# A fused gated linear attention and MLP kernel: another written-out order of its steps

## The chip, the core and the metric

The kernel runs on one core of one Trainium2 chip. The metric is the device time of one execution in microseconds (us). Five engines work side by side, each with its own in-order queue: TensorE (PE) for matrix products, VectorE (DVE) and ScalarE (ACT) for elementwise work, GpSimd (POOL) for small elementwise work, and SyncE (SP), which here issues all DMA transfers. PE takes two instructions for a product, a weight load (PEld) and the product itself (PE); a float32 product takes two such pairs, a bfloat16 product one. A float32 transpose also shows one pair in this kernel's trace.

## What is computed

The reference has two parts. The first is a gated recurrence over 768 tokens, for 4 batches of 8 heads with 48 channels; the second is an MLP with a leaky activation over the resulting 3072 rows.

```python
mag = np.sqrt(a_re * a_re + a_im * a_im)
scale = np.minimum(mag, 0.999) / (mag + 1e-06)
a_re_n, a_im_n = (a_re * scale, a_im * scale)
for t in range(S):
    ar, ai = (a_re_n[:, :, t, :, None], a_im_n[:, :, t, :, None])
    new_re = ar * S_re - ai * S_im
    new_im = ar * S_im + ai * S_re
    kv = np.einsum('bhd,bhe->bhde', k[:, :, t], v[:, :, t])
    S_re, S_im = (new_re + kv, new_im)
    y[:, :, t] = np.einsum('bhd,bhde->bhe', q[:, :, t], S_re)
...
h = x @ w_in                     # x: (3072, 384), w_in: (384, 2048)
g = np.maximum(h, 0.0) + alpha * np.minimum(h, 0.0)
return (g @ w_out).astype(np.float32)   # w_out: (2048, 384)
```

Inputs and output are float32 in the reference's shapes; x is y with its heads laid side by side.

## The kernel before

**Units.** A unit is 128 tokens of one batch with all eight heads. There are 24 units, six for each batch, numbered in order of time within the batch. The recurrence is solved inside a unit by six levels of halving (half lengths 1, 2, 4, ..., 32), and between units by a state St that is passed on.

**Gates.** The function `gates` (nine calls, for one unit, two units, and then three units each) turns the gate inputs into magnitudes ("dec", stored to DRAM as decs) and into products of unit phases ("phs"). It is a long chain of DVE and ACT steps (L251 to L308), of complex products (L336 and L338, small ones of batches 1 to 3 on POOL), and of the last products (L422, L425), which are stored as phs (L427).

**Loads.** `loads` brings KQ (queries and keys of a unit, L575 and L577), PP (its phases, L586) and T (its decays, L593). KQ has three buffers, T two, PP one. `half_rows` and `loads_v` bring the values: a copy to DRAM in another layout (vsc, L556), V (L602 to L607) and VL (L625, L628), with one buffer each.

**A unit's steps** (`unit`). DVE rotates KQ with PP (L648). For each level PE makes 16 small products into ps_lv (`meet`, L662), DVE scales KQ with T for the next level (L701) and masks the result into A (L686, or ACT at L683), and ACT copies half of the keys into W (L719). After the last level PE transposes the keys (L736), ACT copies them (L738), and PE makes the products for the state (ps_kv, L747). Then follow the products for the output ps_y: four bfloat16 products with zeros, which clear the unit's sum (L759), 48 products with A (L768), and, once the state is known, 16 products with St (L793). DVE updates St (L777, L780). ACT copies ps_y (L807) and SP stores it as ysc (L812).

**The MLP** (`all_mlp`). Units are taken in 14 groups: two of one unit, ten of two, two of one. `loads_x` brings a group's rows back as xT (L825). For each of 16 feature blocks, `features` makes three products into ps_h (L841), ACT applies Relu (L848), and DVE adds alpha (L850), which also frees the ps_h buffer (two there are). `outputs` makes one product per unit and feature block into ps_o (L860); after the sixteenth ACT copies it (L870) and SP stores it (L873). Both weights are loaded in sixteen pieces and converted on ACT and DVE (`pieces`, L487; `to_f32`, L503 to L515).

**What sets the order.** Every function above is a generator that stops (`yield`) ahead of each of its steps. A string, ORDER, has one letter for each step, 4,316 in all. The run goes through it and advances the generator that the letter names by one step, so the string alone decides in which sequence every engine's queue is filled:

```python
def run(self, order):
    for c in order:
        next(self.tasks[self.LETTERS.index(c)], None)
```

A to I are the nine gate chains, J loads, K half_rows, L loads_v, M pieces, N and O the weights in and out, P to Z and a to m the 24 units, n loads_x, and o the MLP. The arguments of each `yield` (a cost, what it waits for, which buffers it takes, and for PE a number n of product instructions) were meant for the planner that composed the string; in this kernel they do nothing. That of the step which clears a unit's sum counts 12 products and four clearing ones:

```python
ev = yield PE(0.335 if s or part else 0.44, ..., mode=2, n=12 if s or part else 14)
if not (s or part):
    ...
            nc.tensor.matmul(..., lhsT=nothing[64 * i:64 * i + 64], rhs=ident.bitcast(BF16)[64 * i:64 * i + 64],
                             start=True, stop=False)
```

The waits between engines follow from the data and from the buffers; the order changes none of them, only what stands ahead of what.

Of the kernel before, what the change touches and what calls it, by code (L numbers as in the profile page):

```python
# [27 lines left out]


ORDER = (  # L30
    "AAAAAAAAAAABBBAAAAAAAAAMMMMMJKKNJAAABBNAAAMNNAANKJJAOAAAAAAAAAAAAAAABAAKKKKKKKOBLLAANAAAAAAAOOMLAAAA"
    "BBOKLLLMAAABALABLKBBAAAKAAABBNAABABAAABAABAAAAABBBBBBABABAABNNABBBBBABAABBBBBBBBBBBBOOOBBBNBBNBBBBBN"
    "BMBOBJBBBJPCNNBBCBBBBBBBCOBBBBBBPOBPPBCBLLJJOCONBNBCBMPJJJBJMBOBBLBNBOPBBPBPPBPBBOCCCPCPPCOCPCJJJPPP"
    "PCCPPCCOOJCLOPPLLCOPPCPPCCNDJNCCJNNDPQQDMPPPCMOCOKCPPPPPPPPNCCCCOCJJCMCCNCCCCCCPPKKCJCCQDDCCCCPCQCDC"
    "CPCPPPQPQPPPPKCJNJNCNNCKQCCNCNDOCJCRCCQCCNCDDDCONOOCRQNRCRQQCPQQQCDJKDCCORQCKQDDQCOKCQCCDNCKKQQMCDOQ"
    "nODCLLLLLLLLLQLLQQRLLDCJDOCDMDQoDDKCQCoMoKKKDCLCCCOQQQJQQQDQRQDCQQCQRKJDDDRDDCDCCCCQCOQOCOOOQDoQNDND"
    "oRoooooDMKRDoRRDNDoOooQNDJREoooooJoNRSDQRooRQRRoJNoLLoDoQoooooRJoSQLLERRRDRRooooooDLQLOSLLLNRRDLLLDD"
    "DLDRoooooLDDESSODoESRooRSEooQNQENRoSoNooooooRRRRRRRoSSNRoMRoDoEooSSROOOOooORoooNDNDoODDDNRooDDoDDDDR"
    "JoooJNKJRJJSoooJnTEooooooooooSoLLDTDDDDESSSEoooooooJJJJLLLSSSJJSSJooDJLLooSoooRTooooooDDDLLSooooLLDD"
    "DDDDoLETTDSooTRoSSLKKSooUooooooEoESoooSREELSoSKKKDoTooooooSEoERSKSSSSSDoSooooLDDDSDLDEoDToJLLEDTJLLL"  # L40
    "EooDDDooLooEooooSooSDSSSSSETUToSLooToooLoooDEEoooEEoTLTooooToEoooooToooLLDTToooDTTTTooDnLoooTEEooooD"
    "TUoooToUEDTooooUTToEoooooUTUTJUEEEEEooUoJoEoTJoooUTTJTTTTTTEooTFJUTEFooooooKooTJUUUoULUoooEooEULEooL"
    "LUTUUUUEoULLLLoooUoELoToUUUoEEoEEVEEEooEEEEEFEUVUoLJULooooLTLUJTUVToVVVUUUUUUUUVFVVVooooooVVVVooJoVo"
    "JoJTTUJJUJWVVJLUUUEEEEEEEEEEEEoEoooVJFoJoVooWVUUWooLLLLLLLLWWVoLLLLVEooWWEVoVVVWooooVVWWVoooWVVooVoL"
    "EEVEVonJJoVVVEJVFWVVJWoVEEEEEFFoVJWVoWWFFEKWJJooooLooVVooFXEFJJWEEWooooLLLLLooooWEFWELLLLJELLLWoEEEV"
    "VVVVVWEoooooooWoWWoXoWooooLEWWEWEooooooooWEEooooKWWWWWWJEFXXXXWLWFJXXoooWLLoJoooXLoLFWFFoWWJXXXXLFFo"
    "oooooooJWoooooLLWWFWFLLXFLLFLFLFFXYooooooooXXoWWoooFFFoooXXYoFYXXFFoooXXoooXGooXXFXYFFooooooXXXooYFF"
    "FFFoooXXooooYnXFXFoFoFGFXXXXXoooXoXooYYooJJJoJJJZooYJXXXYJLYXXXFFFJFFXLFFooYYooooFJFZZYYZFKXLYoooooo"
    "oooooZZYYZYFFFFFFYYYoLFLLLZZLLFFFFLFFYFYooooKKooooooYZFoGLYYooYoLLLYJYoJooZYYooFYYFJYYZYYYYKFFFFFJZF"
    "ZYaZGGFFFooZooooooooFoLLooooFoJooooJYFGFZZFFFFYYYYYYYFFaZaoooooFGoooaJZJKJoaGFLooZZFFooooooZZoaoLLaL"  # L50
    "GZZoooooooFLKoFGGGooZZaaZoZoooooGooooGooZoLLLZaGLLaFaoooaGoGGooGoooooJLLZZZZZZZaaHnooooKoGGGGGGGGGGH"
    "aooooaHJJLLLLLLKoooooZZLGGGZaaaGaaaaLLooooooooGGooooKoooHLLLZZGGZZGZZZaboooooooaaJooLooHoGGboaaHaGoG"
    "GoooooJJGooooGooJJaoabHbaaGGabbbJaaGaGGGGGGGGHbJaboHHJbJJooooooGooGcbbbbHHHooooboooooHaaaaaabbHbbGGo"
    "GooaaoooooooobccbooHobbJJGooooooocbboccbobobboobGoHbGGGGGGGGGGbGccoobooobcoHLLLJLLLLLLLLLLLbbbbbbcbc"
    "cGobboooooJGncJJdooLLGLooLcGLooooooGGGGodccccccHooccooccLLKGLGbbbJJLLoLcobbccbbcbooLGooooGGGdccooooo"
    "oooGGGccGGooooLLoooooocJGdcooHcccHGocGHGJJLLdHHHHHLLcHccHoooLodooJooLooddooGooooHHHHHodooooodIdccccH"
    "HooHHHoooooooooHcoddcooooJJocoHdoododHoooHddddHdeddJodooooooLLooooJIoIdeoooLdeeddddeoooooodLcLLooLdL"
    "dneooeeoooooeddddIdKKddHHHHHHHHHdddeoIddeooeooddIJJJJJJfdJJLoeJoooILHHHHHooooLLLLoeooJIIeLLLLLeIoooo"
    "oooeeeffoooooooeeeeeKKooooffefoHeoHoHHeHHHHHHHHHHHfoHeIoHHeoeooIefeLLJfLIIIIIIIIoodoJoHoeeeeeeeoooHJ"
    "JooeeHoooooeegfIKooooHffHfoooooooofJHHHJJJfIfoeeeeeeogfLIooJooooooJfoHHHofoooIooHggHffHHoofffnHogooo"  # L60
    "ooogHLLLLLLLLLLLfffKKHLLHooofoooHHofoooooooooooIIoIffIoIHfooffffHKfKooooofggogoooofffgffLJogJoogohLo"
    "gooohgJJoggoooooooooooooooooooooogLhhLLfggggggffohhhLLoKoooooooogoooooohggIJJooooogJgghhgJoooJhogooL"
    "LLhhLLLhgfgggggJggKffIooohiooooooohgJgIIIiggoggggIIooooIIIIooooooooIIIIIJiooooohiioohoooJIJJJooJoooo"
    "ooooooooLooonoihhooooohhihhoooohhoooooIooIIIIIIIIIIooooooLIIIIIIIIIIIIIIILoLIooLoiihiohiooooohhhhooo"
    "ohiLLLhLJiooLLLLLhhhhhhojohhhIoooooIoIIiiooioooLoLiLiiiiijhhiLJiJLLLjjooLIIIIIIILojILLLoooooijjjoojL"
    "IIILoioIooIoooojooiiIiooiioooojjoioooooooohhhIoojohiiiiiiiiiihhiiiiLLLLLLjIjiojooooioijLLLjIIjIoooIj"
    "jnjoJooLLIjoooooJJJJJLjoooojooooooooooooooooooLjooooojjooojooojooojoooLJJookojojjjjjJjjjjjkkoooookko"
    "oookokooooJJkoJooJJJkkkjJjLLlookkjoooookkkkooooooollkolkLkLLLkklkjoooooooLokojlkkLLLLoLoLLkoookJkooo"
    "kllkolllkkkkkJkkkkkJJJlojooooooljkkJJkoLkLkklolooolkolookJooomooooooooooolllnLLommmmoolllLooooLooooo"
    "ooooooooooooooooLLLLLmmllllloooooooooooloooooolmmoololoooLLLoooooooooooolmoooooooooollllmmlmlmmlmlll"  # L70
    "mLLoooooooooLLooLLolmLLLooLLLlloooooloLomoooooooooooooommmmmmmoommooooooooollnooooooomoomooooooooooo"
    "ooooooooooooommooooooooooooooooooooooooooooooooooooooommmmmmmmmmmmmmmoooooooooooooonoooooooooooooooo"
    "oooooooooooooooooooooooooooooooooooooooooooooooooooooooooooooooooooooooooooooooooooooooooooooooooooo"
    "oooooooooooooooo")

# [877 lines left out]
```

## Time and profile before

| | |
|---|---|
| median of 3 runs | 878.04 us (871.34 to 885.96) |
| the profiled execution | 879.98 us, span 878.3 us |
| PE busy | 712.8 us (81%) |
| DVE busy | 648.2 us (74%) |
| ACT busy | 425.8 us (48%) |
| POOL busy | 167.5 us (19%) |
| mean granted clock of PE | 0.955 |
| DMA | 130.92 MB in 194,559 packets, mean 149 GB/s |
| largest groups | L841 308.0 us, L860 298.4 us, L701 176.8 us |

A page of the profile has the busy time of each engine, then 40 equal slices of the span in which a digit is the busy share in tenths, then the DMA queues, and then groups of instructions by source line ("L841" is line 841). A group's row names the engine, the operation, what is written and read, the count, the busy time, the mean of one in ns, and the idle time just before it with what ended it. "X <- Y" in a row of waits means that X was released by Y; three numbers follow, the sum in us, how often, and the longest. "issue" as the releaser means that nothing the profile shows was waited for. The queue named "instruction" carries the engines' own programs.

### The profile page before, as it was taken

The page shows a single profiled execution, that of the slowest core. Times are in us where ns is not written, and L with a number is a line of the kernel's source. Part 1 is how long each engine was busy: PE and PEld are TensorE (multiplying, and loading weights), DVE is VectorE, ACT ScalarE, POOL GpSimd, SP SyncE. Part 2 cuts the span into 40 slices and gives each one's busy share as a digit, 9 for nine tenths or more (in the row PEclk, how much of TensorE's full clock was granted, in tenths as well). Part 3 has the DMA queues.
Part 4 walks back from the last instruction along what each step waited for, and adds up shares of the span by engine and source line. Part 5 has one row for each costly group of instructions (what it writes and reads, how often), then busy time and mean ns, then how long its engine had stood idle before and what let it go on. Part 6 is the DMA issues. An engine that isn't in the chain of part 4 may idle for free.

```text
span 878.3 us, 26867 instructions
## 1 busy us (share of the span) xinstructions
PE 712.8 (81%) x11488; PEld 534.3 (61%) x11488; DVE 648.2 (74%) x1012; ACT 425.8 (48%) x913; POOL 167.5 (19%) x277
## 2 busy tenths in 40 slices
PE   0001325788979998979999999999999979999998
PEld 0001324567757776757776776777777766777776
DVE  5999999888977998769987896885756737624212
ACT  7587693666344653536673446543334314233121
POOL 3000002363132310520073105810032000000000
PEclk9999755999998999999999999999999999999999
DMA  8698869886984989447976678659544392712010
GB/s 225 187 240 201 229 155 286 191 169 124 252 165 88 172 181 235 102 94 203 213 139 132 166 187 158 135 153 212 119 90 98 92 212 47 157 31 65 10 38 9
DMA packets 194559, 130.92 MB, mean 149 GB/s; under 512 B 74504, under 2 KB 186248, under 8 KB 194440
## 3 DMA queue, kind: packets, MB, share of 16 engines
q1 hardware_dynamic: 194440, 129.20, 64.6%
q8 instruction: 90, 1.47, 0.7%
q14 instruction: 29, 0.24, 0.1%
HBM read 100.82 MB, written 35.71 MB: 155 GB/s over the span
## 4 chain that ended last, share of the span: by engine, by line
PE 63%; DVE 9%; DMA 8%; ACT 5%; issue 4%; SPq 3%; POOL 2%; DVEq 0%; POOLq 0%; ACTq 0%
PE ps_h L841 25%; PE ps_o L860 25%; PE ps_lv L662 4%; PE ps_y L768 3%; PE ps_y L793 2%; DVE KQ L701 2%; PE ps_kv L747 2%; DMA PP<-phs 2%; SPq L625 1%; PE ps_kt L736 1%; DMA T<-decs 1%; DMA VL<-vsc 1%; DMA g_sb<-in_w_in_dram 1%; POOL gate L336 1%; DMA phs<-gate 1%
## 5 line engine op out<-in xcount | busy, mean ns | idle before, releaser
L841 PE MATMUL ps_h<-xT,w_in_sb 128*128 128x256 f32 (+1 forms) x1344 | 308.0, 360 | 5.6 <-DVE g_sb L850 5.1
L860 PE MATMUL ps_o<-w_out_sb,g_sb 128*128 128x384 f32 x768 | 298.4, 502 | 10.3 <-DVE g_sb L850 10.1
L841 PEld LDWEIGHTS ps_h<-xT,w_in_sb 128*128 128x128 f32 x1344 | 234.2, 195 | 76.9 <-DVE g_sb L850 7.5
L701 DVE TENSOR_TENSOR KQ<-KQ,T 96x1024 f32<-96x1024 f32 x144 | 176.8, 1235 | 58.9 <-PE ps_lv L662 55.6
L850 DVE SCALAR_TENSOR_TENSOR g_sb<-g_sb,al,ps_h 128x256 f32<-128x256 f32 (+1 forms) x224 | 97.2, 436 | 135.8 <-ACT g_sb L848 135.6
L848 ACT ACTIVATE g_sb<-ps_h 128x256 f32<-128x256 f32 (+1 forms) x224 | 78.7, 352 | 243.9 <-PE ps_h L841 242.8
L860 PEld LDWEIGHTS ps_o<-w_out_sb,g_sb 128*128 128x128 f32 x768 | 139.1, 193 | 61.1 <-DVE g_sb L850 11.8
L719 ACT COPY W<-KQ 96x512 f32<-96x512 f32 x120 | 74.7, 624 | 70.3 <-DVE KQ L701 62.0
L662 PE MATMUL ps_lv<-KQ,W 96*32 96x32 f32 x3840 | 57.2, 205 | 49.9 <-ACT W L719 44.4
L662 PEld LDWEIGHTS ps_lv<-KQ,W 96*32 96x32 f32 x3840 | 44.8, 117 | 78.2 <-ACT W L719 51.0
L648 DVE TENSOR_TENSOR KQ<-KQ,PP 96x2048 f32<-96x2048 f32 x24 | 55.2, 2300 | 10.4 <-DMA PP<-phs 5.1
L662 PE MATMUL ps_lv<-KQ 96*32 96x32 f32 x768 | 12.2, 208 | 62.1 <-DMA VL<-in_v_dram 51.3
L768 PE MATMUL ps_y<-A,VL 64*48 64x64 f32 x2304 | 44.4, 226 | 21.5 <-issue 18.7
L336 POOL TENSOR_TENSOR gate<-gate 128x72 f32<-128x72 f32 x42 | 25.6, 609 | 160.9 <-ACT gate L366 158.1
L768 PEld LDWEIGHTS ps_y<-A,VL 64*48 64x48 f32 x2304 | 41.1, 127 | 23.4 <-issue 20.0
L662 PEld LDWEIGHTS ps_lv<-KQ 96*32 96x32 f32 x768 | 9.7, 120 | 66.2 <-DVE KQ L648 51.8
L336 DVE TENSOR_TENSOR gate<-gate 128x576 f32<-128x576 f32 (+5 forms) x84 | 47.6, 566 | 1.6
L683 ACT ACTIVATE A<-ps_lv,rows 128x64 f32<-128x64 f32 x144 | 40.0, 330 | 16.0 <-PE ps_lv L662 15.6
L807 ACT COPY yT<-ps_y 48x256 f32<-48x256 f32 x96 | 32.0, 365 | 30.9 <-PE ps_y L793 24.7
L422 DVE TENSOR_TENSOR gate<-gate 128x1152 f32<-128x1152 f32 (+2 forms) x36 | 43.5, 1218 | 0.4 <-POOL gate L407 0.3
L686 DVE TENSOR_TENSOR A<-ps_lv,mask 128x256 f32<-128x256 f32 x96 | 39.4, 413 | 0.0
L738 ACT COPY KT<-ps_kt 128x384 f32<-128x384 f32 x48 | 22.9, 478 | 24.5 <-PE ps_kt L736 24.3
(100 smaller groups left out, 771.8 us busy)
## 6 DMA issues: line engine op xcount, KB each, us to landing
T<-decs SPq DMA_DIRECT2D x48, 384.0 KB
PP<-phs SPq DMA_DIRECT2D x48, 193.5 KB
KQ<-in_q_dram SPq DMA_DIRECT2D x48, 192.0 KB
decs<-gate SPq DMA_DIRECT2D x7, 1152.0 KB
phs<-gate SPq DMA_DIRECT2D x14, 576.0 KB
KQ<-in_k_dram SPq DMA_DIRECT2D x40, 192.0 KB
vsc<-in_v_dram SPq DMA_DIRECT2D x48, 144.0 KB
VL<-vsc SPq DMA_DIRECT2D x24, 288.0 KB
```

The lines of the kernel that those rows point to most:

```text
L336: on(4 * k).tensor_tensor(out=m, in0=w[:, 1::-1].unsqueeze(2).to_broadcast([P, 2, 2, k]), in1=pairs_of(u), op=ALU.mult)
L422: TT(out=m[:, a], in0=U5[:, 1 + a], in1=turned(off3, o)[:, a].unsqueeze(1).unsqueeze(3).to_broadcast([P, L // 2, nb, 2]), op=ALU.mult)
L648: nc.vector.tensor_tensor(out=KQ, in0=KQ, in1=bass.AP(tensor=PP.tensor, offset=PP.offset, ap=[PP.ap[0], (1, 2), (P + 1, H), (1, P)]), op=A ...
L662: nc.tensor.matmul(t[64 * i + j:64 * i + j + HC // 2, p], lhsT=weights(4 * i + p)[:, j:j + HC // 2], rhs=q_[:, m * g:m * (g + 1)], start=T ...
L683: nc.scalar.activation(a[:, :, cols], t[:, :, at:at + name], AF.Copy, scale=s)
L701: nc.vector.tensor_tensor(out=x, in0=x, in1=m, op=ALU.mult)
L719: nc.scalar.copy(W.rearrange("p n t -> p (n t)").rearrange("p (m h) -> p m h", h=h), halves(KQ[:, 1].rearrange("p n t -> p (n t)"), h)[:, ...
L768: nc.tensor.matmul(o, lhsT=Vp[h][64 * i:64 * i + 64, s, e_ * D:(e_ + 1) * D], rhs=a, start=False, stop=False)
L841: nc.tensor.matmul(p, lhsT=w_in_sb[:, f // 2, kk, f % 2 * P:(f % 2 + 1) * P], rhs=x_of[m][:, kk], start=(kk == 0), stop=(kk == NK - 1))
L848: nc.scalar.activation(gt, p, AF.Relu, scale=-1.0)
L850: nc.vector.scalar_tensor_tensor(out=gt, in0=gt, scalar=al_1[:, f:f + 1], in1=p, op0=ALU.mult, op1=ALU.add)
L860: nc.tensor.matmul(sums[0], lhsT=gt[:, c * P:(c + 1) * P], rhs=w_out_sb[:, f], start=(f == 0), stop=(f == NF - 1))
```

## The change

Only the string ORDER differs. Both strings have 4,316 letters, and every letter occurs as often in one as in the other, so the kernel makes the same instructions on the same data with the same buffers. The new string is the order found anew, with one PE instruction counted, where two had been, for each of the bfloat16 products that clear a unit's sum (L759; four for each unit). The source line of that count is the same in both files. The first and the last lines of the difference:

```diff
 ORDER = (
-    "AAAAAAAAAAABBBAAAAAAAAAMMMMMJKKNJAAABBNAAAMNNAANKJJAOAAAAAAAAAAAAAAABAAKKKKKKKOBLLAANAAAAAAAOOMLAAAA"
-    "BBOKLLLMAAABALABLKBBAAAKAAABBNAABABAAABAABAAAAABBBBBBABABAABNNABBBBBABAABBBBBBBBBBBBOOOBBBNBBNBBBBBN"
-    "BMBOBJBBBJPCNNBBCBBBBBBBCOBBBBBBPOBPPBCBLLJJOCONBNBCBMPJJJBJMBOBBLBNBOPBBPBPPBPBBOCCCPCPPCOCPCJJJPPP"
-    "PCCPPCCOOJCLOPPLLCOPPCPPCCNDJNCCJNNDPQQDMPPPCMOCOKCPPPPPPPPNCCCCOCJJCMCCNCCCCCCPPKKCJCCQDDCCCCPCQCDC"
-    "CPCPPPQPQPPPPKCJNJNCNNCKQCCNCNDOCJCRCCQCCNCDDDCONOOCRQNRCRQQCPQQQCDJKDCCORQCKQDDQCOKCQCCDNCKKQQMCDOQ"
-    "nODCLLLLLLLLLQLLQQRLLDCJDOCDMDQoDDKCQCoMoKKKDCLCCCOQQQJQQQDQRQDCQQCQRKJDDDRDDCDCCCCQCOQOCOOOQDoQNDND"
...
+    "AAAAAAAAAAAAAAAAAAAAABBJBAAMMMMKMAAAAAAANNBAAAAAAAAAAAAAAABNBMAAAJAAAAAAAAAAJJBANALBABAABANBBBOBABBAB"
+    "AABAAAAKAOBNABKKMBBOBBOKBBBLLLAOABBLLLLLLABMLLBABANAAAAABOABABNAAABAKBAABNNOBBBNBBBONOMLBBBBOBOBBBBB"
+    "BBNBBBBNNBOBBNBBNOOOBBBBOBCBJJPCBBBBBBOBMCCCOPBJBJCBMJNBPMBNNPPBBBJPKKKKKKKKBBBCBBCBOCKCBCBCCCCPCPCK"
+    "BPCPPOPJJJLJCCPNJJPNPCDDCCCCPPCPOCONCQPCOPCQPPPQPPPQPCPPQCQOCJPJPPJPPMJJNPNNNCQCQQCCOOPPPPPCPOCPCNCP"
+    "PPCPNCOPCPPCJMQQLPCCQQCDCOJPCCNNMLDCONCCCCCNCCNJKMCMnKKRCCCKORNCNCJCRLJJDCCCRCCCCQCOOOCCRRCCQCOCOOMO"
+    "COOCRRooooNCNKKoCooNooOKCOCLKKMKoKKDCoooCCCCooQQQQKCooRQQCCQQNQQooQDooDDLLCNoooCDQQCQoQoooooRoooQDDQ"
...
+    "ooooooomoLllmmLLLooooooooolooooooooooollloooolloooomLoLoLLLLLllllllmlmmmoomoooooooooooooollmooooolll"
+    "lllmomlmmmmmLooooooooLLoLLLoooLLLooLooooooooooooooooooooooooooooooooolnooooooomooooooooooooooooomooo"
+    "ooooooooooooomoooomoomooooLooLLoomooooooooommooommmmmmmmmmmmmmmnoooooooooooooooooooooooooooooooooooo"
     "oooooooooooooooooooooooooooooooooooooooooooooooooooooooooooooooooooooooooooooooooooooooooooooooooooo"
     "oooooooooooooooo")
```

The first n (the load of the first group's xT) is the first letter of the sixth line before, and stands in the middle of the fifth line after; the first o that makes a product follows it.

More of the change, by code (lines that the diff above doesn't have):

```diff
@@ L36 @@
-    "nODCLLLLLLLLLQLLQQRLLDCJDOCDMDQoDDKCQCoMoKKKDCLCCCOQQQJQQQDQRQDCQQCQRKJDDDRDDCDCCCCQCOQOCOOOQDoQNDND"
[L37 to L70, printed above, removed]
@@ L71 @@
-    "mLLoooooooooLLooLLolmLLLooLLLlloooooloLomoooooooooooooommmmmmmoommooooooooollnooooooomoomooooooooooo"
-    "ooooooooooooommooooooooooooooooooooooooooooooooooooooommmmmmmmmmmmmmmoooooooooooooonoooooooooooooooo"
+    "AAAAAAAAAAAAAAAAAAAABBJBAAMMMMKMAAAAAAANNBAAAAAAAAAAAAAAABNBMAAAJAAAAAAAAAAJJBANALBABAABANBBBOBABBAB"
+    "AABAAAAKAOBNABKKMBBOBBOKBBBLLLAOABBLLLLLLABMLLBABANAAAAABOABABNAAABAKBAABNNOBBBNBBBONOMLBBBBOBOBBBBB"
+    "BBNBBBBNNBOBBNBBNOOOBBBBOBCBJJPCBBBBBBOBMCCCOPBJBJCBMJNBPMBNNPPBBBJPKKKKKKKKBBBCBBCBOCKCBCBCCCCPCPCK"
@@ new lines @@
+    "BPCPPOPJJJLJCCPNJJPNPCDDCCCCPPCPOCONCQPCOPCQPPPQPPPQPCPPQCQOCJPJPPJPPMJJNPNNNCQCQQCCOOPPPPPCPOCPCNCP"
+    "PPCPNCOPCPPCJMQQLPCCQQCDCOJPCCNNMLDCONCCCCCNCCNJKMCMnKKRCCCKORNCNCJCRLJJDCCCRCCCCQCOOOCCRRCCQCOCOOMO"
+    "COOCRRooooNCNKKoCooNooOKCOCLKKMKoKKDCoooCCCCooQQQQKCooRQQCCQQNQQooQDooDDLLCNoooCDQQCQoQoooooRoooQDDQ"
+    "DDRLLLLLLLLDDDoDoRQRDDDCQDQDQQQRDQRJQQQEEooooRDRoooRQNEJJJoQQNQQJJQDDLDDDDSDRDROoEoooooooESSRDSDooRo"
+    "NoDERRoNRoDoSDREEooooSDLLLooEDooooRRoSLLLRDDDDRooORRDDSDDEQLLLLLLLRSRDRRNRRRRDSRDDDDODDooooDDDDEoNES"
@@ new lines @@
+    "oJooooOSSNJJEoJRJRRRSSTLLLLLLLLooSSoooOoJRRKDDJRoELSTnOTTToSKKoDDDoooooTLoSDDDDDDDDDoSSSSoRLToEooKoT"
+    "oSoooooSSoSooooooooTETDEooSLoSSLLoETDDDEDDDooooooDSoooSSSSSSTSoSJTSoDEJJEJJEKJDoooLJLDoDLLEDEEoLoSSE"
+    "SSSSSTSoooJoUoTEEEEooDDooToDooooEooooooooTnLDDooooDooooooooDEUTooooooJJLDDJooooDoooEoooooooooUTooToo"
+    "oLLLLLooTDTETLooooooUTEooUoTTEoDUoooTEoEUTLooTKooEUEToJToToooUETTTTTTTETEEEETJEEEFJFETUoLoUUooooooUV"
+    "TLUoFoToooTTLLUUooLoToUooVFVoUoUUUUoUUoooooFoJJUUVLLTULLLLLLoooVEEEUFUVooUUUEEEooTooEEEEEEEEEEEUUVUU"
@@ new lines @@
+    "UJUVUVEEFooVEooooJJJJJWVooEEEEEJUoUUUVooWUVJVoUVWKWJUoUVoEVEVWoVEEJoEEEoJWWWoJJJoVVVoWVooooVWEWVVnoL"
+    "LLLLoVXLLLLooooLLLEEFLVFELEEEEFoEoVooooooVVoEoWEoVoooVoooVVVVVVVVWVEVLWWWooooooJoFFWVFWWEWXFooVVWWEV"
+    "WooVLLJLJVooooooooooLLLLLVFWEWWFWWFoooooooWooooVWWoooWLLLLLWWWWWoFXXFXXWEWWoFoWFXXJFJJJJLYXFoooooooo"
+    "XFXXoFFFFKJJWGoWWWXooooFooooYYWYXGWWWFoXFooYXFXoooooFoYXXXYFooYFFGFoooooooooXXooYXXooXYGooFXooFXFFXo"
+    "oooXXGooXXFFFoFFLnooGoGJYoGLLLLLLLLLLLLXXXXXFFFXXFFFFXFFXJYJJJJZoGoooKooYoGooJoooooooooGGoYXZYYGYFFF"
@@ new lines @@
+    "FFFFFFGGJZFoZoFoooZoooGGooooXYYYYXXYZZZooYYLFLLLLLLooLLLFFoLoLLZooooXXYKKFFFFYYFFZYoooooGYYoFooFFFYF"
+    "LoFGYGGGFooKoJJJKKFGGGGoYYYYYYYYYJXZooooKZoJJaKKKooLFFFooZZZLoJoZLLLooFGJLLLLXLLoLoKGFFFFoFFoooooooG"
+    "GGYFYZaZaaZZooZZooooGaZZFLLFJFoooooooYYYYYYooaaFoaooooaoooJooJooZaZZZaooooZoooFZnZGGaooaoGooGGooZZZZ"
+    "ZZZZaZZZGJJJHaaGJbbHooooooooooooooobGaGoZGZZaaaaaJLJJabGGHZoGZZZJJbooooooGGGooGooooaLooJboaabbHHboLL"
+    "ooooaboaHbLaooaooooooHooLLLoLLooLaaLLoooGGooGGbaaGGaaGGaaooGoaJGoGGGGGGGGGGGHabbcLLHaHbGcbHHHHJJJboo"
@@ new lines @@
+    "ooooooooJJboooobLLGGocoobobJoooobcGGGcbbbboooHoHGbccbcKJJLLLLGoooooaocLdHaLooaobaGGbcLbLKLooGGLabbba"
+    "ooooooobbGbbcHbGbbboocncoooHbGGGGGGGooocHHbodoooJJoLLoHLLoLLGGGLLLGLLHoooooLLoHooHoHoooooccKdooooooH"
+    "HHHHGoooooHHooodoGLHcdoocccccobbbbbbHbdJdooGooooHoodHcHdoooooooocccddocoHHHodHHJcJJJoooJcoooccocIooo"
+    "odHccccccoHccdIcoodeoHJoHoodooHHHHdodHddddHccccHJeLcLJcoooLJLLLeooooooooddooccLeLJoHHooHeHHHHHHHHedd"
+    "dLIeoLooodooHHddooooLLdoLLoJJdeHHHdddddIIdddonoILJodoeoooooeLooILLfoooHHHHHHoeeooJooJIooKKoooooeHHfd"
@@ new lines @@
+    "dfIfodLeoeLKeKfoKKoeoodoLddIdLJJffLLLLLLeeofoeeIoofeooeooooIeooIofHHIJHHIdoIIeeooJoooHHHooeKHHoIIeoe"
+    "ooeeeofHHoooeHHHHeeeeeIHLILLoooeIoeJeJJffooooooooooooKeoffgJffooooooIIoooooooooLLHHooIHHIIIfeeeeegoo"
+    "ofoooeegooooooooLfffffooooooofgfggJooofLfJooLfooLLfLKHgLofLLgoofogJoffffffffIgffnooogogooJJJhIIIIooL"
+    "oooIIhogoohJoooohIgLfJffLLgooooofffoIggoooooooooohLhLLLIgghgIggJLgLLgJooIooooggohgoIoIghofoooooohhgI"
+    "IogoIIhgooohooooooLIIILIggggggggIJJhJooJhhgLLLhhiohoooooooIIoooohhhhhooooohohJooJgIIIIIIhhLLLIIIILhI"
@@ new lines @@
+    "IiooLooggooggihhhIoiooogoooooohIIIILIgJLLLLLoohoooooioIIooIIIIoIoohhohhhhhhihJoJnJiiiJJJJooooooooohI"
+    "IIIIIIiooIjooIIoIIioiooIoooIIIooooojijiiooooooooLoojiooooIoojhLiILLiLLIoLoooiiiiJoLLooLooohLhooooIho"
+    "ihhihjjooiooooiioiijjoooiiojiLLLioiiiioooJJJjjiiiioooLoooJjjioojjojJokooooooooojjikiiijjjJJkLoooijoo"
+    "oookokkjjLkoooLookojkojkoojiijjnooookojoooooooookjLLLoLooLLLLLLjjjjjJJJkJJjJLoooooLLLLLoojjjoooooooo"
+    "ooooolJJLoooollLjjjkjjojkkloooooooooooooooljjLkkkkklkLkllkJooooooooooolllkLklkJJLJLoooooolLkooookook"
@@ L73 @@
+    "kkooooooookkkkkkkkkJJoomooooooookkmkkkloollooooooJJokmooookknloooooooooommlmLoollmlLlloooooooloLoooo"
+    "ooooooomoLllmmLLLooooooooolooooooooooollloooolloooomLoLoLLLLLllllllmlmmmoomoooooooooooooollmooooolll"
+    "lllmomlmmmmmLooooooooLLoLLLoooLLLooLooooooooooooooooooooooooooooooooolnooooooomooooooooooooooooomooo"
+    "ooooooooooooomoooomoomooooLooLLoomooooooooommooommmmmmmmmmmmmmmnoooooooooooooooooooooooooooooooooooo"
     "oooooooooooooooooooooooooooooooooooooooooooooooooooooooooooooooooooooooooooooooooooooooooooooooooooo"
```

## The prediction

> **What bounds the kernel now.** I read the slices of the span first, then stretches chosen from them, then the waits of TensorE in the late stretch, then the timeline around the longest ones. The slices and the queues:
>
> ```profile
> PE 712.8 (81%) x11488; PEld 534.3 (61%) x11488; DVE 648.2 (74%) x1012; ACT 425.8 (48%) x913; POOL 167.5 (19%) x277
> PE   0001325788979998979999999999999979999998
> DVE  5999999888977998769987896885756737624212
> ...
> PEclk9999755999998999999999999999999999999999
> ...
> q8 instruction: 90, 1.47, 0.7%
> ```
>
> VectorE (DVE) is full from the second slice to the seventh, while TensorE (PE) has little to do; from about slice 18 on PE is full. Busy time of the engines by stretch (columns: stretch and length, PE, PEld, DVE, ACT, POOL, clock, DMA share, GB/s):
>
> ```profile
> 0.00:66.00 66.00, 1.31 (x64) 1.04 (x64) 54.91 (x156) 47.88 (x75) 8.80 (x32) 1.00 0.88 217
> 66.00:154.00 88.00, 31.05 (x862) 25.75 (x863) 87.35 (x146) 58.34 (x88) 6.77 (x7) 0.71 0.83 218
> 154.00:200.00 46.00, 34.16 (x650) 26.55 (x652) 37.92 (x59) 30.68 (x68) 24.66 (x32) 0.96 0.82 172
> 200.00:396.00 196.00, 177.92 (x3196) 133.99 (x3193) 160.54 (x218) 95.20 (x220) 53.01 (x87) 0.96 0.72 158
> 396.00:878.00 482.00, 468.38 (x6731) 346.97 (x6730) 307.45 (x437) 193.71 (x466) 74.23 (x120) 0.99 0.55 121
> ```
>
> PE idles 64.7 + 57.0 + 11.8 = 133.5 us before 200 us, where DVE sets the pace, and 18.1 + 13.6 us after it, of which some 4 us are the last copy and store. Only the order changes, so PE's work stays what it is; the end moves by what PE's idle time moves. In the late stretch PE waits for:
>
> ```profile
> PE ps_y L768 <- issue: 13.1, 6, 4.1
> PE ps_h L841 <- DVE g_sb L850: 5.1, 1, 5.1
> PE ps_y L793 <- issue: 3.6, 3, 2.1
> PE ps_lv L662 <- ACT A L683: 2.9, 1, 2.9
> PE ps_lv L662 <- issue: 2.4, 3, 1.7
> PE ps_lv L662 <- ACT W L719: 1.9, 6, 0.5
> ```
>
> The largest sum is "issue", 13.1 + 3.6 + 2.4 = 19.1 us: PE waited for nothing that a semaphore explains. The longest of these, in PE's timeline:
>
> ```profile
> 716.11 1.15 PE L747 MATMUL ps_kv<-V,KT 64*64 64x48 f32 x64
> 717.07 0.29 PE L759 MATMUL ps_y<-ident,KT 64*48 64x256 bf16 x4
> 717.18 1.29 PE L768 MATMUL ps_y<-A,VL 64*48 64x64 f32 x77
> 722.60 0.54 PE L768 MATMUL ps_y<-A,VL 64*48 64x64 f32 x19 [4.12 <-issue]
> ```
>
> It falls inside a run of equal products. In the trace's DMA records, the 76th packet of the instruction queue (16,384 bytes) started at 719.95 us and took 1.21 us; PE went on 1.4 us later. Counting PE's instructions (weight loads, products, semaphore instructions) in the trace, each of the long issue waits ends at instruction 256j + 193, just after packet j landed; and no packet starts earlier than about instruction 256j - 100. So a packet has roughly 290 instructions in which to come. In a unit's closing run (L747, L759, L768, L793) those are 2 to 5 us of PE time.
>
> **What the Trainium skill says.** "Runtime: NRT & Kernel Launch", section "Instruction fetch mechanics": each engine's instruction memory is a FIFO "refilled in 16 KiB blocks" of 256 instructions, over a DMA queue of its own, at a cost "mostly hidden". The trace agrees on the block (90 packets of 16 KiB), not on the cost: 19.1 us after 200 us are not hidden. "DMA: Bandwidth & Descriptors", section "Issuing engines are not separate DMA queues": all DMAs share 16 engines. That fits the time from the earliest possible start of a packet to its landing: median 3.6 us, up to 13.8 us where the DMA share is high, though a packet itself takes about 1.2 us.
>
> **The change, part by part.** I applied both orders to the generators and counted what stands ahead of what; durations are those of the trace of before. Nothing is added or removed: the same 4,316 steps.
>
> *Instruction blocks.* PE's distance between products of one kind, from back-to-back runs: L841 0.215 us (256 columns) or 0.12 (128), L860 0.323, L768 0.016, L747 0.015, L662 0.0125, L793 0.036, L736 0.084. With these I sum PE's work between instructions 256j - 100 and 256j + 193. From block 61 on, the order of before has five windows under 5.5 us, two of them of 2.3 us (blocks 73 and 76; the 4.12 us wait is block 76's); the new order has one, of 5.2 us. For blocks 37 to 60 it is two against three, for 13 to 36 five against five. The drift has a cause in the counts: L759 is one record a product (96 in all), the others two, so an order composed with two records for L759 places block ends 4 x 2 = 8 instructions (weight load and product) off for each unit, 160 at unit 20. Late blocks gain their two waits, 4.12 + 0.54 us: **-4**. Early ones: as many short windows in the same DMA load, 0.
>
> *Cover between levels.* Between the level products of a unit (L662) PE needs other work while DVE (L701, 1.24 us) and ACT (L719, 0.62 us) prepare the next level: 1.9 us. Of the gaps of units 4 to 23, twelve hold under 2 us of PE work before, four after. The waits they explain are 1.9 + 2.9 us (the rows of ACT W and ACT A); a third to two thirds go: **-2**.
>
> *The front.* DVE's queue sets it. The first hidden product's L850 stands behind 153 us of DVE work before, 127 after; at 155 us of DVE work PE has been given 15.2 us of work before and 21.7 after, but at 185 us 36.1 against 37.1, at 245 us 84.5 against 86.7. So the earlier start is largely given back before PE saturates: **-2**. Unit 0's first step stands 6 us later in DVE's queue (43 to 49 us), that of units 3 and 4 at 161 to 161 and 188 to 191: nothing to be had from there.
>
> *Unit 11's wait.* The 5.1 us of L841 come from DVE, whose queue is stopped in front of unit 11's L648 while PP, issued late on SP, arrives:
>
> ```profile
> 373.62 0.48 SPq L586 DMA_DIRECT2D PP<-phs  x1
> 380.29 2.29 DVE L648 TENSOR_TENSOR KQ<-KQ,PP 96x2048 f32<-96x2048 f32 x1 [4.91 <-POOL gate L403]
> ```
>
> Behind L648 stand the L850 that free PE's hidden sums. The row names POOL; the transfer, landing some 6 us after issue, is the likelier cause. In the new order the distance from PP's issue to L648 is 2 us of DVE work (3 before): this stall can stay, go, or arise at another unit. Between 0 and -5: **-2.5**.
>
> *Loads and xT.* On SP's queue the load of KQ stands closer to its use (unit 9: 19 us of DVE work to 2; unit 18: 25 to 2; but unit 13: 7 to 14). A late load stops DVE as above; from none to one more stall of 5 us: **+1.5**. From a group's last L793 to its first L841 the chain of L807, ysc and xT needs about 11 us (group 10: 691.7 to 703.6, with 0.5 us of idle left). PE's work in between is at least 10.2 us before; after, group 3 has 9.3 instead of 15.4: **+1**. The last stretch, after unit 23, is equal to three hidden products: 0.
>
> Sum: -4 - 2 - 2 - 2.5 + 1.5 + 1 = **-8 us** on the profiled execution, 879.98 us (span 878.3 and 1.7 around it): 872. That execution is 1.9 us above the median of the runs shown (878.04; 871.34 to 885.96), so I forecast **870** for a median. About 2% (17.6 us) is what a measurement of this kernel can tell from no change.
>
> **Rivals.**
> 1. *Larger gain.* Nearly all late idle goes: 19.1 us of issue, 5.1 behind L850 and 4.8 between levels are 29; with two thirds of that, 19, and 2 from the front, 878 - 21 = **857**. For it: windows and covers are longer in the new order. Against it: as many short windows in blocks 13 to 60, where 14 of the 19 us lie.
> 2. *Nothing.* A fetch's delay is set by what the DMA engines hold at that moment; other short windows (blocks 43 and 51, 4.4 and 5.0 us) stall in place of 73 and 76, and closer loads take the rest: **878**. Against it: late packets land in about 2.7 us.
> 3. *Slower.* PE's queue is stopped in the front. The first L841 now follows unit 0's end by 127 - 101 = 26 us of DVE work (153 - 103 = 50 before). The trace shows unit 0's L793 at 101.7, the issue of xT at 118.5 us, after weight pieces on SP's queue, and the landing some 4 us later (an estimate, from the 3.7 us of an ysc transfer in the chain of waits): 21 us. Behind the L841 stand unit 1's level products, for which DVE waits. It decides from 5 us of further delay; one more weight piece in front of xT is 8.3 us (that DMA's step in the chain of waits), two are 16.6, less 5 of slack 11.6 of idle DVE, less 2 of other gains: **888**.
> That the change doesn't do what it says can't move the time apart from these, since only the order counts.
>
> **How the numbers follow.** Forecast 55% (864 to 876), first rival 17% (849 to 863), second 18% (876 to 883), third 10% (884 to 900). Range: 855 leaves out about a tenth in the first rival, 885 about a tenth in the third. Faster by over 2% (below 860.5): most of the first rival, 0.16. Slower by over 2% (above 895.6): 0.03 of the third. Within: 0.81.
>
> **What would show it.** PE's issue waits from 700 us on gone, those before 400 us about as large; first L850 near 125 us rather than 148; PE's idle to 200 us at 131 or so; rows of L662 on ACT below 3 us. I am wrong if DVE shows a gap before 154 us, if L648 waits at several units, or if issue waits appear in new closing runs.

## The result, and the profile after

The changed kernel takes 864.02 us in the median of 20 runs (858.51 to 874.73), the kernel before 878.92 us (869.41 to 886.76, 20 runs); the ratio is **0.9855**, with a 95% interval of 0.9825 to 0.9885. Ratios leave out runs that lie over 1.5% above the fastest of the same kernel, so they are not the quotients of these medians (0.983 here). The forecast was 870 us, the range 855 to 885. The profiled execution spans 863.5 us against 878.3.

First the same rows of the page of the kernel after:

```profile
PE 707.2 (82%) x11488; PEld 528.3 (61%) x11488; DVE 649.0 (75%) x1012; ACT 427.4 (50%) x913; POOL 172.2 (20%) x277
PE   0001425777999899999899999998999999999998
DVE  5989999897988989999679977977748655532212
...
PEclk9999957789999999999999999999999999999999
...
q8 instruction: 90, 1.47, 0.8%
```

The picture is that of before; what differs is within tenths, so the same five stretches follow (columns as in the prediction: stretch, length, busy time of PE, PEld, DVE, ACT and POOL, clock, DMA share, GB/s):

```profile
0.00:66.00 66.00, 0.66 (x32) 0.52 (x32) 53.24 (x156) 48.51 (x74) 9.64 (x32) 1.00 0.83 208
66.00:154.00 88.00, 34.82 (x910) 28.15 (x912) 85.42 (x141) 60.43 (x92) 0.37 (x4) 0.79 0.87 216
154.00:200.00 46.00, 30.40 (x606) 23.13 (x603) 39.38 (x60) 29.16 (x57) 19.77 (x28) 0.83 0.77 173
200.00:396.00 196.00, 185.05 (x3287) 138.09 (x3287) 179.15 (x240) 107.46 (x244) 69.45 (x98) 0.99 0.77 172
396.00:864.00 468.00, 456.25 (x6663) 338.40 (x6661) 291.85 (x419) 181.87 (x449) 72.97 (x116) 0.99 0.54 121
```

PE's idle time up to 200 us is 65.3 + 53.2 + 15.6 = 134.1 us, against 133.5 before: nothing was won in the front. From 200 to 396 us it is 10.95 us against 18.1, after that, to the end of the span, 11.25 against 13.9. That makes 9.2 of the 14.8 us by which the two profiled spans differ. The other 5.6 us are in PE's busy time, 707.2 against 712.8, with the very same instructions. The trace points to the clock: PE was busy for 46.4 us at half clock before and for 36.3 after. In a slow spell before, products of L860 follow one another at 640 ns instead of 323, so 10.1 us less of that is worth some 5 us (an estimate). In the stretch from 200 to 396 us the granted clock is 0.99 against 0.96. After 204 us the trace's clock records hold 20.5 us at half clock before, in five spells, each begun during or right after a long wait of PE, and 6.8 us in two spells after. PE's waits from 200 us on:

```profile
PE ps_h L841 <- DVE g_sb L850: 5.6, 2, 3.8
PE ps_o L860 <- issue: 3.0, 3, 2.3
PE ps_lv L662 <- issue: 2.9, 3, 1.9
PE ps_o L860 <- ACT top L870: 1.9, 1, 1.9
PE ps_y L793 <- issue: 1.7, 1, 1.7
```

"issue" has fallen from 19.1 us to 3.0 + 2.9 + 1.7 = 7.6 us, and L768, which had 13.1 of it, is no longer in it. In e10, a second trace of the changed kernel, the sum is 7.5 us. Of the waits that end at the fixed place, instruction 256j + 193, there are eight of 0.5 us or more before (17.8 us) and three after (6.0 us). Unit 20's closing run, which broke off for 4.12 us before, now goes through. The place where PE would stop for block 76 has moved from the 77th of the L768 products to about the ninth, and the time from instruction 256j - 100 to it has grown from 2.4 to 9.4 us:

```profile
701.26 1.15 PE L747 MATMUL ps_kv<-V,KT 64*64 64x48 f32 x64
702.23 0.29 PE L759 MATMUL ps_y<-ident,KT 64*48 64x256 bf16 x4
702.34 1.55 PE L768 MATMUL ps_y<-A,VL 64*48 64x64 f32 x96
```

### The profile page after: what moved, and what is told of

Same layout as the page of the kernel before. It is cut to its first block, busy times and chain, and to the rows that moved or that the text cites. A ratio compares the mean times of both kernels' runs of the same rounds, so it can differ in the third digit from the quotient of the medians.

```text
span 863.5 us, 26876 instructions
## 1 busy us (share of the span) xinstructions
PE 707.2 (82%) x11488; PEld 528.3 (61%) x11488; DVE 649.0 (75%) x1012; ACT 427.4 (50%) x913; POOL 172.2 (20%) x277
## 4 chain that ended last, share of the span: by engine, by line
PE 61%; DVE 16%; DMA 11%; issue 3%; SPq 3%; POOL 3%; ACT 2%; DVEq 0%; ACTq 0%; POOLq 0%
PE ps_h L841 24%; PE ps_o L860 24%; DMA T<-decs 5%; PE ps_lv L662 4%; DVE KQ L701 4%; PE ps_y L768 3%; PE ps_kv L747 2%; DMA phs<-gate 2%; PE ps_y L793 2%; DVE gate L336 2%; POOL gate L336 1%; PE ps_kt L736 1%; SPq L625 1%; DVE gate L422 1%; DVE gate L338 1%
## 5 line engine op out<-in xcount | busy, mean ns | idle before, releaser
L841 PE MATMUL ps_h<-xT,w_in_sb 128*128 128x256 f32 (+1 forms) x1344 | 308.7, 361 | 8.3 <-DVE g_sb L850 5.6
L860 PE MATMUL ps_o<-w_out_sb,g_sb 128*128 128x384 f32 x768 | 296.9, 501 | 13.4 <-DVE g_sb L850 6.6
L841 PEld LDWEIGHTS ps_h<-xT,w_in_sb 128*128 128x128 f32 x1344 | 235.0, 196 | 78.9 <-DVE g_sb L850 8.5
L850 DVE SCALAR_TENSOR_TENSOR g_sb<-g_sb,al,ps_h 128x256 f32<-128x256 f32 (+1 forms) x224 | 97.3, 437 | 120.3 <-ACT g_sb L848 119.7
L860 PEld LDWEIGHTS ps_o<-w_out_sb,g_sb 128*128 128x128 f32 x768 | 138.1, 193 | 66.4 <-DVE g_sb L850 11.2
L662 PE MATMUL ps_lv<-KQ,W 96*32 96x32 f32 x3840 | 56.4, 205 | 50.4 <-ACT W L719 44.4
L662 PEld LDWEIGHTS ps_lv<-KQ,W 96*32 96x32 f32 x3840 | 44.6, 117 | 76.0 <-ACT W L719 52.5
L662 PE MATMUL ps_lv<-KQ 96*32 96x32 f32 x768 | 12.2, 208 | 71.2 <-DVE KQ L648 55.5
L648 DVE TENSOR_TENSOR KQ<-KQ,PP 96x2048 f32<-96x2048 f32 x24 | 56.3, 2344 | 12.8 <-DMA PP<-phs 12.7
L336 POOL TENSOR_TENSOR gate<-gate 128x72 f32<-128x72 f32 x42 | 29.6, 705 | 153.8 <-ACT gate L366 151.0
L662 PEld LDWEIGHTS ps_lv<-KQ 96*32 96x32 f32 x768 | 9.7, 120 | 75.0 <-DVE KQ L648 55.5
L768 PE MATMUL ps_y<-A,VL 64*48 64x64 f32 x2304 | 41.4, 224 | 5.2 <-DMA VL<-vsc 4.0
L768 PEld LDWEIGHTS ps_y<-A,VL 64*48 64x48 f32 x2304 | 39.5, 125 | 5.7 <-DMA VL<-vsc 4.2
L807 ACT COPY yT<-ps_y 48x256 f32<-48x256 f32 x96 | 31.3, 365 | 20.4 <-PE ps_y L793 19.1
L780 DVE TENSOR_TENSOR St<-St,ps_kv 96x384 f32<-96x384 f32 x44 | 24.1, 548 | 15.3 <-PE ps_kv L747 12.4
```

The costliest lines, as they stand in the source:

```text
L336: on(4 * k).tensor_tensor(out=m, in0=w[:, 1::-1].unsqueeze(2).to_broadcast([P, 2, 2, k]), in1=pairs_of(u), op=ALU.mult)
L648: nc.vector.tensor_tensor(out=KQ, in0=KQ, in1=bass.AP(tensor=PP.tensor, offset=PP.offset, ap=[PP.ap[0], (1, 2), (P + 1, H), (1, P)]), op=A ...
L662: nc.tensor.matmul(t[64 * i + j:64 * i + j + HC // 2, p], lhsT=weights(4 * i + p)[:, j:j + HC // 2], rhs=q_[:, m * g:m * (g + 1)], start=T ...
L768: nc.tensor.matmul(o, lhsT=Vp[h][64 * i:64 * i + 64, s, e_ * D:(e_ + 1) * D], rhs=a, start=False, stop=False)
L841: nc.tensor.matmul(p, lhsT=w_in_sb[:, f // 2, kk, f % 2 * P:(f % 2 + 1) * P], rhs=x_of[m][:, kk], start=(kk == 0), stop=(kk == NK - 1))
L850: nc.vector.scalar_tensor_tensor(out=gt, in0=gt, scalar=al_1[:, f:f + 1], in1=p, op0=ALU.mult, op1=ALU.add)
```

## The experiments

Each ratio below is to runs of the kernel before on the same chip (e1 to e8 on one, e9 to e11 on a second, e12 on a third). A trace is of one execution, and waits of the same steps differ between traces: block 20's, 3.48 us before, is 1.11 in e7, 0.87 in e8 and 0.87 in e12, which change nothing up to there. In kernels whose order string takes one more line of the file, line numbers are one higher (L769 for L768).

### Do the ends of the instruction blocks matter? (e1, e2)

The theory from the prediction: PE waits where a packet of 256 instructions comes late, so that time depends on where in the order the block ends fall. The rival: the gain comes from waits on data. Products of zeros ahead of everything, while PE has nothing to do, move every block end and no step:

```diff
+        Y0 = ps.tile([P, 2, 512], F32, tag="y", name="ps_y")[:, :, 0:2 * P]
+        for n_ in range(16):            # e2, in the changed kernel: 64
+            e_, i = n_ // 2 % 2, n_ % 2
+            nc.tensor.matmul(Y0[64 * e_:64 * e_ + D, i], lhsT=nothing[64 * i:64 * i + 64],
+                             rhs=ident.bitcast(BF16)[64 * i:64 * i + 64], start=True, stop=True)
         plan.run(ORDER)
```

> The changed kernel, with 64 more such products ahead of everything: block ends fall 128 instructions earlier. No step moves. By count, the windows under 4 us of PE work rise from none to 15 (blocks 13 to 90). Fetch theory: new issue waits of 1 to 4 us at many closing runs, 10 to 30 us in all, so 875 to 895 us, ratio to before 0.995 to 1.02. Rival (waits on data): as the changed kernel, 864 us, ratio 0.985.

e2: 902.94 us, ratio **1.0256** (1.0208 to 1.0303), beyond even what the fetch theory gave. Between the two ratios, 1.0256 and 0.9855, lie 4%: 64 tiny products in an idle stretch cost some 35 us (4% of 879). PE's waits from 200 us on:

```profile
PE ps_y L769 <- issue: 22.3, 11, 3.5
PE ps_lv L663 <- issue: 8.7, 5, 3.4
PE ps_y L794 <- issue: 4.2, 1, 4.2
```

That is 35.2 us of issue instead of 7.6. After 204 us eleven slow spells hold 51.2 us, against 6.8 in two, and PE's busy time after 200 us is 661.2 us against 641.3. Each long issue wait again ends at instruction 256j + 193 (or the next), now counted with the added ones. This part of the theory stands: the new order's gain rests on where its block ends fall, and at this other place it is lost.

> The kernel before, with 16 more bfloat16 products of zeros put ahead of everything on PE, while PE has nothing to do: no step moves, but every end of a block of 256 PE instructions falls 32 instructions earlier in the order. By count, the two windows of 2.3 us of PE work between the earliest start of a block's packet and the point where PE needs it (blocks 73 and 76) become 4.8 us or more; elsewhere as many short windows stay. Fetch theory: the issue waits of 4.12 us at 722.6 us and 0.54 us at 751 us go, with the slow-clock spell behind the first: 871 to 875 us, ratio 0.991 to 0.996. Rival (the gain of the new order comes from waits on data, that is from which loads and steps stand ahead of which): nothing moves, 878 us, ratio 1.000.

e1: ratio 0.9916 (0.9886 to 0.9946). That is in the expected range, but it counts only 13 of the 22 runs; the medians of all are 876.40 us and 879.92 before, a ratio of 0.996, between the two theories. So the size decides nothing here. The trace, of an execution of 878.49 us, does: in unit 20's closing run the wait that should have gone is still there:

```profile
712.16 1.15 PE L747 MATMUL ps_kv<-V,KT 64*64 64x48 f32 x64
713.13 0.29 PE L759 MATMUL ps_y<-ident,KT 64*48 64x256 bf16 x4
713.24 1.06 PE L768 MATMUL ps_y<-A,VL 64*48 64x64 f32 x61
718.93 1.30 PE L768 MATMUL ps_y<-A,VL 64*48 64x64 f32 x35 [4.63 <-issue]
```

Block 76's window had become longer as counted: PE passed instruction 256j - 100 at 708.9 us and stopped at about 714.3. But the packet started only at 716.2 us. So a window of 5.4 us is not enough; something holds the packet back. What e1 gains, if anything, is not located: block 31's wait of 2.84 us has gone and block 20's has fallen from 3.48 to 0.55, but block 20's is as small in traces that leave it alone.

### What holds the packet back? (e7)

In the kernel before, SP issues T of unit 21 (two of 384 KB) and KQ of unit 22 (four of 192 KB) between 709.7 and 712.9 us, just ahead of the closing run that begins at 716.1. e7 moves unit 22's loads, on SP alone, behind unit 20's closing run; PE's sequence and block ends stay. In SP's queue:

```diff
   J 593 (21), J 593 (21)                      # T of unit 21
-  J 575, J 577, J 575, J 577 (22)             # KQ
-  J 586, J 586, J 593, J 593 (22)             # PP, T
   L 602, L 604 (21)                           # V, behind unit 20's L747
+  J 575, J 577, J 575, J 577 (22)
+  J 586, J 586, J 593, J 593 (22)
   L 607 (21)
```

> The kernel before with one move on SP alone: the eight loads of unit 22 (KQ, PP, T), issued from 710.8 us on just ahead of unit 20's closing run, are issued after the first two V loads of unit 21, which wait for that run's L747. PE's sequence is untouched: block 76 keeps its 2.3 us of PE work. If the 4.12 us wait is a packet of instructions queued behind these loads, it shrinks to 1 us or less and the slow-clock spell behind it goes: 870 to 874 us, ratio 0.990 to 0.995. If the shortness of the block's window alone makes the wait (a lone packet took 3.6 us in the middle), it stays at 1.5 to 4 us: 876 to 879 us, ratio 0.997 to 1.001.

e7: 873.56 us, ratio **0.9941** (0.9915 to 0.9968). The closing run:

```profile
712.71 1.15 PE L748 MATMUL ps_kv<-V,KT 64*64 64x48 f32 x64
713.68 0.29 PE L760 MATMUL ps_y<-ident,KT 64*48 64x256 bf16 x4
713.79 1.55 PE L769 MATMUL ps_y<-A,VL 64*48 64x64 f32 x96
```

With a window as short (2.1 us; 2.4 before) the wait is gone: the packet started at 712.06 and had landed at 713.14 us. In e12, which has this move too, it is gone as well; in e8, which has not, it is 4.40 us. So what made the wait of block 76 is the bulk loads issued just ahead of it; the short window only left no room. Block 73 agrees: its window is as short (2.3 us by the prediction's count), but before the change its packet started at 687.85 and landed at 688.83 us, and PE did not wait.

### Unit 11's wait (e8), and both moves (e12)

The row of the wait named POOL, the prediction took the late PP. e8 issues it earlier, again on SP alone:

```diff
   o 873
+  J 575, J 577, J 586, J 586 (11)             # second half of KQ, PP
   L 625 x7 (9), K 556 x2, L 625 x3 (9), L 628 (9)
-  J 575, J 577, J 586 (11)
   K 556
-  J 586 (11)
```

> The kernel before with one move on SP alone: the second half of unit 11's KQ and its PP are issued ahead of ten VL loads and two vsc loads of unit 9's group instead of behind them, some 9 us earlier. If unit 11's late PP is what stops DVE at L648 and through it PE (5.10 us in front of L841, and a slow-clock spell after it), that wait falls under 1 us: 871 to 874 us, ratio 0.991 to 0.995. If POOL's L403, which the row names, is the cause, nothing moves: 878 us, ratio 1.000.

e8: 873.71 us, ratio **0.9949** (0.9924 to 0.9974). Unit 11's rotation starts 9 us earlier, without a wait, and the 5.10 us in front of L841 have gone:

```profile
371.10 2.28 DVE L649 TENSOR_TENSOR KQ<-KQ,PP 96x2048 f32<-96x2048 f32 x1
```

It was the transfer, not POOL.

> The kernel before with both moves of loads on SP: unit 22's loads behind unit 20's closing run, and unit 11's PP ahead of the VL loads. If the two waits are independent, the two ratios (0.9941 and 0.9949) multiply: 0.989, 868 to 870 us; that is two thirds of what the changed kernel gains without any step moved on PE, DVE, ACT or POOL. If a later wait takes back what an earlier one gives, as the middle of the span seemed to show after PP's move: 0.993 to 0.996, 872 to 875 us.

e12: 865.13 us beside 875.65, ratio **0.990** (0.9864 to 0.9935). This is what the product of the two ratios gives (0.989); the other forecast, 0.993 to 0.996, is only touched by the interval's end. Two moves of loads on SP's queue give 1.0%, about two thirds of the changed kernel's 1.45%; by the intervals it can be less than half or nearly all.

### The front or the rest? (e3, e4, and again e10, e11)

Two strings of 4,316 letters, each the first part of one order and then what is left, in the other's order:

```diff
-ORDER = before
+ORDER = before[:1043] + (after, without the steps done)   # e3; cut at about 218 us
+ORDER = after[:1032] + (before, without the steps done)   # e4
```

> The order of before up to its 1043rd step (about 218 us), then all steps that are left in the new order. Loss theory from the two traces: of PE's time lost (time gone by less the work done), the new order loses 4 us more than the old one before 200 us and gains 14 us between 200 and 396 us and some 4 us later; so this keeps the gains and drops the loss: 860 to 863 us, ratio 0.979 to 0.983. Rival (the front of the new order is what makes its later gains, with more hidden products given early): 868 to 876 us, ratio 0.988 to 0.997.

> The new order up to its 1032nd step (about 218 us), then all steps that are left in the order of before. Loss theory: only the front's loss is kept: 880 to 884 us, ratio 1.002 to 1.006. Rival (the front makes the gain): 864 to 872 us, ratio 0.985 to 0.993.

e3: 862.96 us, ratio 0.9801 (0.9753 to 0.985). e4: 893.27 us, ratio 1.0128 (1.0085 to 1.0171), slower than both theories had it: right at the seam, at 242.6 us, PE waits 10.56 us for xT of group 2, whose load the seam puts behind the VL loads of the other order. Less those 10.56 us it would be 882.7 us, in the range of the loss theory, but a slow spell of 13.65 us also begins in that wait, so e4 decides little. By e3 the gain comes with the rest: with the old front it is all there. Whether the old front is better than the new one was tried again beside the changed kernel:

> The changed kernel, beside the other two: 864 to 867 us, ratio 0.984 to 0.988.

> The order of before up to its 1043rd step and the new order after it, once more, beside the changed kernel: if the front is worth the 4 to 6 us that the traces show at 200 us, 860 to 863 us, ratio 0.979 to 0.983, clear of the changed kernel. If the front does not matter: as the changed kernel.

e10, the changed kernel: 860.15 us, 0.9816 (0.977 to 0.9862). e11, e3 again: 861.15 us, 0.9825 (0.9773 to 0.9878). No difference is seen. Nor is the old front's lead certain: PE idles for 128.1 us up to 200 us in e10's trace and for 130.0 in e11's.

### Loads of one order, compute of the other (e5, e6)

```diff
-ORDER = before
+ORDER = before's A-I, O, N, P-Z, a-m, o, with J, K, L, M, n where after has them   # e5
+ORDER = after's A-I, O, N, P-Z, a-m, o, with J, K, L, M, n where before has them   # e6
```

A load was set where as much PE and DVE work had gone by, as far as every pair of steps that both orders have the same way round allowed.

> All steps of the gates, units and MLP in the order of before; the steps that only load (KQ, PP, T, V, VL, vsc, raw weights, xT) set among them by where the new order has them. PE's instruction sequence, and so every end of a block, is that of before. Theory L (the gain comes from when the loads are on the DMA engines: instruction packets and PP then come in time): 864 to 870 us, ratio 0.983 to 0.990, issue waits after 200 us under 12 us. Theory C (the gain comes from what stands beside what on PE, DVE and ACT): 876 to 882 us, ratio 0.997 to 1.003.

> The opposite mixture: all compute steps in the new order, the loading steps where the order of before has them. Theory L: the gain goes: 873 to 882 us, ratio 0.994 to 1.004. Theory C: 862 to 868 us, ratio 0.981 to 0.988.

e5: 909.5 us, ratio 1.0368 (1.0325 to 1.0412). e6: 895.24 us, ratio 1.0184 (1.0139 to 1.0229). Both missed both theories. PE waits in e5 from 200 us on:

```profile
PE ps_h L842 <- DMA xT<-ysc: 16.4, 3, 11.4
PE ps_y L769 <- DMA VL<-vsc: 12.3, 7, 3.9
PE ps_o L861 <- DVE g_sb L851: 6.1, 2, 5.6
PE ps_lv L663 <- issue: 2.7, 3, 1.2
```

The issue waits are small (5.1 us in all), as theory L had it, yet xT and VL now come late. In e6, where theory L would have had the issue waits back, they are 3.0 us, and PE waits 14.1 us for L851 and 10.9 for xT. The mixtures don't tell loads from compute; they show that here the loads of either order go badly with the compute steps of the other.

### A further version (e9)

```diff
-  H 248, H 248 (gate loads) ahead of b 706 (St of unit 12)
+  b 706, then H 248, H 248
-  I 321 (store of decs) ahead of L 602, o 873
+  L 602, o 873, then I 321 and the three steps of I after it
```

> The order of before up to its 1043rd step and the new order after it, with two further moves: the loads of gate chain H go behind the load of unit 12's St, which DVE waited for with L850's products queued behind it (PE idle 4.34 us), and the store of decs of chain I (1,152 KB) goes behind unit 16's closing run, whose block 62 waited 3.51 us for its packet. If both waits are transfers queued behind these: 4 to 8 us and part of two slow-clock spells less than that kernel without them (0.980): 854 to 859 us, ratio 0.972 to 0.977. If not: ratio 0.980.

e9: 864.33 us, ratio 0.9861 (0.9817 to 0.9904). No gain. Its profiled execution ran at a granted clock of 0.586 throughout and can't be read against the others, so where the two waits went is open.

## Why the prediction was right, and where not

The time, the sign and the bound are as forecast; the sum of -8 us was a bit over half of the 14.9 us that the medians differ by. That it came so near is in part luck: the terms for the front, unit 11 and the loads, which add up to -2, were each about 0 or not borne out. By its steps:

- **Instruction blocks, -4.** The mechanism held and the size did not; this is the largest term, and the most under-sized. Issue waits after 200 us fell by 19.1 - 7.6 = 11.5 us. Of the two late waits, that of 4.12 us went as forecast, though one of 2.33 us came at block 62. The other, of 0.54 us, was misread: the trace puts it down to VL, and it ends at 256j + 183. The early ones, put at 0 for "as many short windows in the same DMA load", fell from 14.8 to 5.3 us (up to 570 us). In three more traces with the old order they are 9.8 to 11.7 us (e7, e8, e12), in a second one of the new 5.5 (e10), so a fall remains. The new order moves the loads too, and e7 shows for block 76 what that can do. Whether it did so for the early blocks was not tested: issue waits are small in e5 and e6 alike, so neither loads nor compute alone is shown as the cause. Windows did count: e2, with 15 short ones, has 35.2 us of issue. The drift of 8 instructions for each unit that the step gave as a cause was tested by no run.
- **A wait's price.** I took a wait at its length. The Trainium skill, "TensorE: Matmul & The Clock Gate", section "What's actually happening", says that an idle window of about 3.4 us halves PE's clock. The trace agrees in the length of the slow spells, 3.41 or 6.83 us, and in that they begin during or soon after long waits. But a shorter wait can do: spells followed waits of 1.98 us (468.3) and 2.33 us (586.4, after the change), and none one of 2.09 us (534.4). After 204 us the spells hold 20.5 us before and 6.8 after, a cost that no step had.
- **Cover between levels, -2.** Over-sized. The 2.9 us of the row of ACT A are one wait that ends at 199.9 us, not in the late stretch; after the change one of 4.4 us on ACT W ends at 199.1. Without them the rows of L662 on ACT fell from 1.9 to 0.9 us. That the cover did it was not isolated by a run.
- **The front, -2.** Not borne out. PE's idle time to 200 us rose by 0.6 us between the two traces, but it scatters by more: 125.6 to 133.5 us in six traces with the old front (before, e3, e7, e8, e11, e12), 134.1 and 128.1 in two with the new one. e11 against e10 shows no effect at the end. The first L850 did come at 126 us instead of 148, so an earlier start alone gave nothing that could be seen.
- **Unit 11, -2.5.** The cause was read rightly against its row (e8). But the row stands at 5.6 us in the new order too: 3.85 us of it at 424.6 us, not long after DVE had stopped 2.3 us for unit 12's PP and 2.4 us for its St. The term was about 0.
- **Loads and xT, +2.5.** DVE waited longer for PP, 12.7 us in seven waits, but PE had other work; PE's waits on xT are 0.7 us against 0.5. The term was about 0. Two signs that the prediction had named for being wrong did appear, L648 waiting at several units and DVE gaps ahead of 154 us (1.8 and 1.2 us for T and PP at 62.8 and 86.0 us), without the loss that they were to show.

Of the rivals, the larger gain (857 us) is nearly as close to 864 us as the forecast (7 us against 6), since the issue waits fell by almost as much as it had supposed. No gain (878) lies outside the interval. The slower one, PE stopped at the first L841 for xT, did not come: after the change PE's waits on xT are 0.7 us in the whole span.

## What to carry to other kernels

Where PE idles in the middle of a run of small products and no semaphore explains it, count PE's instructions: if such waits come at a fixed place in each 256, the program itself is late. Moving bulk loads away from the dense run can then help with no step on PE moved (0.6% in e7). An order that is good in this respect is so for its exact instruction count; adding instructions in an idle stretch can cost far more than they take (e2). Compare waits in more than one trace before explaining a difference of a few us. A stall of PE is worth more than its length if the clock drops with it.

## What had not been expected

- 64 products of zeros in idle time cost about 4% (ratio 1.0256 against 0.9855).
- Instructions come over a queue of their own, but a packet of 1.2 us waited from 708.9 us, the earliest it might have started, to 716.2 us, while 1.3 MB of other packets started (e1).
- One move of eight loads, with nothing else changed, gave 0.6%, one of four loads 0.5%.
